# Order edges in the attention stage: weight sums behind a residual addition, two layer norm squares behind accumulator copies

## The chip, the cores and the metric

The kernel runs on one core of one Trainium2 chip. The metric is the time of one execution in device microseconds; every number called a time below is a median of several executions. The profile's own span of one execution is about 1.8 us shorter than its time (739.5 us against 741.27 us for the profiled run before), and its time axis starts at its first instruction. All runs used here are of the undisturbed ("fast") state.

## The reference, cut to what matters

A transformer block: layer norm, linear attention with 32 heads, an output projection added to the input, a second layer norm, and a gated ReLU MLP added again. S = 2048 tokens, D = 1024, F = 3584, all bf16.

```
x = A_x
h  = x + attention(layernorm(x), wqkv, wo)          # out = num / den, then @ wo
h2 = h + relu_gated_mlp(layernorm(h), W_gate, W_up, W_down)
```

## The kernel before

The kernel has three long stages that run into each other on TensorE (PE in the profile): k, v and most of the q projection (0 to 150 us), attention for 16 tiles of 128 tokens with the rest of the q projection (to 207 us) and the first MLP products between them (150 to 290 us), and the rest of the MLP (290 us to the end). All large products use Strassen's scheme: 7 products instead of 8, for which sums of the operands are made ahead on VectorE (DVE), and intermediate accumulators are copied out of PSUM (the memory, in banks, into which PE accumulates) by ScalarE (ACT).

The change touches the middle stage. Tiles are numbered 0 to 15 in the order in which they are worked on. For each, `nd` makes numerators and denominators and divides them (DVE, o_sb), a DMA transposes the result, `wo_h` multiplies by wo (PE, "attn") and adds x (DVE, line L560, one addition for each half); then the second layer norm needs the sum of squares (ACT, "square", L570), is applied (L574), and a DMA transposes the result (hn). For tiles 4 to 7 and 12 to 15 DVE then makes the "left sums" (L117 to L120), which the MLP's Strassen products need. L12 is line 12 of the kernel's own file; the change inserts lines, so that L727 of the kernel before is L729 after, and L736 is L738.

```python
def snap(v, nm, bank=A):                     # in strassen(): accumulator bank v to SBUF
    ...
    with tc.high_priority():
        nc.scalar.copy(out=snaps[nm, v], in_=bank[v][:])          # ACT, L154
...
for j in range(2):                           # in wo_h(): 8 attn matmuls, then
    with tc.high_priority():
        nc.vector.scalar_tensor_tensor(out=h_sb[...], in0=ps[:], scalar=1.0, in1=h_sb[...],
                                       op0=ALU.mult, op1=ALU.add, accum_out=tot[:, j:j + 1])   # L560
...
nc.vector.tensor_scalar(out=nmean, in0=tot[:, 0:1], scalar1=tot[:, 1:2], ...)                   # sm, L568
nc.scalar.activation(out=st["hn"][:], in_=h_sb[:], func=ACT.Square, bias=nmean, ...)            # L570
...
LAG = (0, 1, 1, 2, 4)                        # nd, oT, x_in, wo_h, hn_T of tile n: step n + LAG
def attn_step(step): ...                     # also left_sums(...) for tiles 4-7 and 12-15
...
flow = [...]                                 # four early MLP "quads", six pieces each
for step in range(QSTEPS + 2, ready):
    if step == QSTEPS + 2:
        flow.pop(0)()                        # the first quad's first product
    attn_step(step)
late_sums.pop()()                            # the first quad's eight weight sums (DVE, tg and tu)
for n in range(steps):
    attn_step(ready + n)
    for p in flow[...]:
        p()
```

An early quad multiplies two weight tiles (tg/wg and tu/wu, "v" = 0 and 1) by hn. Its products go to two A banks, two E banks and one D bank. Product m1 goes to A; its copy must be out before m6 is accumulated into the same bank; the same holds between m7 (copy "u3") and m4.

What each engine executes, and in which order, is decided by a scheduler at compile time from priorities and expected times. An order edge tells that scheduler "this instruction behind that one". Between two instructions of one engine it puts no semaphore into the program.

## Time and profile before

| | before |
|---|---|
| time, median of 3 runs at the prediction | 740.93 us (740.51 to 741.72) |
| span of the profiled execution | 739.5 us |
| PE busy | 724.0 us, 98% |
| waits of PE in 120 to 300 us, listed | 3.4 us |

The head of the profile's page of the kernel before: busy microseconds of each engine, share of the span, number of instructions.

```profile
span 739.5 us, 10552 instructions
PE 724.0 (98%) x3967; PEld 382.7 (52%) x4020; DVE 563.7 (76%) x992; ACT 321.5 (43%) x580; POOL 5.6 (1%) x44
```

PE is the bound: only its idle time can be won. (53 of its 4020 matmul records are missing from this trace, which is why a group of four sometimes shows as x3.) The list of waits of PE between 120 and 300 us, kernel before: who waited for whom, microseconds in total, times, longest.

```profile
PE attn L557 <- DVE o_sb L534: 1.0, 3, 0.5
PE Aq L727 <- ACT m L154: 0.9, 1, 0.9
PE attn L557 <- DVE x_res L560: 0.7, 1, 0.7
PE nd L527 <- DVE o_sb L534: 0.5, 1, 0.5
PE Aq L727 <- ACT u L154: 0.3, 1, 0.3
```

The second and the last line are the targets of the edges on the squares. The timeline of ACT, kernel before (start, duration, engine, line, operation, output<-input, and in brackets the idle time before it and what ended it):

```profile
261.57 0.59 ACT L154 COPY m<-Aq 128x512 f32<-128x512 f32 x1 [2.71 <-PE Aq L727]
263.31 1.15 ACT L570 ACTIVATE hn<-x_res,sm 128x1024 bf16<-128x1024 bf16 x1 [1.15 <-DVE sm L568]
264.36 0.19 ACT L570 ACTIVATION_READ_ACCUMULATOR hn<-x_res,sm 128x1 f32 x1
264.45 0.56 ACT L154 COPY m<-Aq 128x512 f32<-128x512 f32 x1
...
273.04 0.59 ACT L154 COPY u<-Aq 128x512 f32<-128x512 f32 x1 [4.88 <-PE Aq L727]
274.18 1.15 ACT L570 ACTIVATE hn<-x_res,sm 128x1024 bf16<-128x1024 bf16 x1 [0.56 <-DVE sm L568]
275.24 0.19 ACT L570 ACTIVATION_READ_ACCUMULATOR hn<-x_res,sm 128x1 f32 x1
275.33 0.56 ACT L154 COPY u<-Aq 128x512 f32<-128x512 f32 x1
```

In both places a square stands between the copies of the two banks and waits for a small DVE operation; the second copy, whose data are there, waits behind it. The timeline of PE over the same time, kernel before:

```profile
263.09 1.03 PE L727 MATMUL Aq<-hs,tg 128*128 128x512 f16 x4
265.07 1.02 PE L727 MATMUL Aq<-hs,tu 128*128 128x512 f16 x4 [0.95 <-ACT m L154]
...
273.70 1.03 PE L727 MATMUL Aq<-hn,tg 128*128 128x512 bf16 x3
274.80 0.81 PE L727 MATMUL Eq<-hs,wg 128*128 128x512 f16 x3
275.95 1.02 PE L727 MATMUL Aq<-hn,tu 128*128 128x512 bf16 x4 [0.34 <-ACT u L154]
```

The matmuls at 265.07 and 275.95 are those that waited for the late copies. And DVE, kernel before, around the weight sums: the second x addition of tile 7, the first weight sum, and the first x addition of tile 8.

```profile
206.46 0.68 DVE L560 SCALAR_TENSOR_TENSOR x_res<-attn,x_res 128x512 bf16<-128x512 f32 x1
...
209.00 0.42 DVE L636 TENSOR_TENSOR tg<-wg 128x512 f16<-128x512 bf16 x1
...
212.35 0.69 DVE L560 SCALAR_TENSOR_TENSOR x_res<-attn,x_res 128x512 bf16<-128x512 f32 x1
```

### The profile page before, as it was taken

What the parts mean: (1) busy time and instruction counts of PE and PEld (TensorE: products, weight loads), DVE (VectorE), ACT (ScalarE), POOL (GpSimd) and SP (SyncE); (2) the same over time, 40 slices, a digit from 0 to 9 for tenths busy, and PEclk for the clock granted to TensorE, in tenths of its full rate; (3) what the DMA queues carried; (4) which work ended last, traced back from release to release, by engine and by line L of the source; (5) the groups of instructions that cost most, each with busy time, mean ns of one, the idle gap of its engine ahead of it and who ended that gap; (6) DMA issues with size and microseconds to landing.
All of it is one profiled execution on the core that took longest, in us unless ns stands there. A gap on an engine that the chain in (4) does not pass through costs nothing.

```text
span 739.5 us, 10552 instructions
## 1 busy us (share of the span) xinstructions
PE 724.0 (98%) x3967; PEld 382.7 (52%) x4020; DVE 563.7 (76%) x992; ACT 321.5 (43%) x580; POOL 5.6 (1%) x44
## 2 busy tenths in 40 slices
PE   8999999999999999999999999999999999999997
PEld 3444555444444444444444444444444458888566
DVE  5997644676798767778778777877786479996797
ACT  4877554778887644434344444444445120000000
POOL 0000000000000000000000000000000000000000
PEclk9999999999999999999999999999999999999999
DMA  9666002169987426164638359575583399987822
GB/s 315 153 145 170 1 1 67 48 149 218 237 168 181 124 73 206 43 193 134 198 117 242 110 177 283 171 219 194 170 277 121 129 398 339 331 288 299 295 76 82
DMA packets 146594, 132.02 MB, mean 179 GB/s; under 512 B 50928, under 2 KB 128112, under 8 KB 146544
## 3 DMA queue, kind: packets, MB, share of 16 engines
q1 hardware_dynamic: 135536, 123.30, 55.4%
q10 hardware_dynamic: 11008, 8.06, 3.4%
q8 instruction: 31, 0.51, 0.3%
q14 instruction: 19, 0.16, 0.1%
HBM read 79.95 MB, written 39.85 MB: 162 GB/s over the span
## 4 chain that ended last, share of the span: by engine, by line
PE 78%; DVE 8%; ACT 7%; DMA 5%; issue 1%; SPq 0%; DVEq 0%; POOL 0%; ACTq 0%
PE accA L821 22%; PE accY L821 8%; PE accX L821 8%; PE accA L1153 8%; PE Aq L314 3%; PE accA L982 3%; PE attn L557 3%; PE accX L1153 3%; PE Aq L454 3%; PE accY L1153 2%; DMA hn<-hn 2%; ACT hn L570 2%; PE Eq L314 2%; PE accY L982 2%; PE accX L982 2%
## 5 line engine op out<-in xcount | busy, mean ns | idle before, releaser
L831 ACT ACTIVATE gu<-gu 128x512 bf16<-128x512 bf16 x72 | 45.4, 631 | 131.4 <-DVE gu L830 131.4
L826 ACT COPY snap<-accA 128x1024 f32<-128x1024 f32 x72 | 72.5, 1008 | 36.4 <-PE accA L821 36.3
L821 PEld LDWEIGHTS <-tu 128*128 128x128 f16 x384 | 37.6, 98 | 45.3
L821 PEld LDWEIGHTS <-tg 128*128 128x128 f16 x384 | 37.6, 98 | 45.3
L557 PE MATMUL attn<-wo_mem,oT 128*128 128x512 bf16 x247 | 58.1, 379 | 2.3 <-DVE o_sb L534 1.0
L830 DVE TENSOR_TENSOR gu<-accY,snap 128x1024 bf16<-128x1024 f32 x36 | 43.9, 1220 | 10.0 <-ACT snap L826 10.0
L821 PE MATMUL accA<-hn,tu 128*128 128x512 f16 (+1 forms) x192 | 49.3, 379 | 0.0
L821 PE MATMUL accA<-hn,tg 128*128 128x512 f16 (+1 forms) x192 | 49.3, 379 | 0.0
L830 DVE TENSOR_TENSOR gu<-accX,snap 128x1024 bf16<-128x1024 f32 x36 | 43.9, 1219 | 6.3 <-PE accX L821 3.7
L154 ACT COPY u<-Aq 128x512 f32<-128x512 f32 x54 | 31.1, 580 | 36.2 <-PE Aq L314 19.3
L1153 PEld LDWEIGHTS <-x 128*128 128x128 f16 (+1 forms) x448 | 43.8, 98 | 5.5
L821 PEld LDWEIGHTS <-wg 128*128 128x128 bf16 x288 | 28.2, 98 | 34.0
L821 PEld LDWEIGHTS <-wu 128*128 128x128 bf16 x288 | 28.2, 98 | 34.0
L557 PEld LDWEIGHTS <-oT 128*128 128x128 bf16 x256 | 24.6, 97 | 32.2 <-issue 4.1
L834 DVE TENSOR_TENSOR hq<-gu 128x512 bf16<-128x512 bf16 x48 | 20.3, 423 | 14.3 <-ACT gu L831 14.2
L314 PEld LDWEIGHTS <-xT 128*128 128x128 bf16 (+1 forms) x192 | 18.6, 98 | 23.8 <-issue 2.4
L534 DVE TENSOR_TENSOR o_sb<-nd,rd 128x384 bf16<-128x384 f32 (+1 forms) x48 | 23.2, 509 | 8.6 <-ACT rd L533 6.6
L1153 PEld LDWEIGHTS <-xs 128*128 128x128 f16 x280 | 27.4, 98 | 3.2
L982 PEld LDWEIGHTS <-x 128*128 128x128 bf16 (+1 forms) x168 | 16.5, 98 | 19.6
L560 DVE SCALAR_TENSOR_TENSOR x_res<-attn,x_res 128x512 bf16<-128x512 f32 x32 | 22.0, 686 | 6.1 <-PE attn L557 5.9
L1159 DVE TENSOR_TENSOR snap<-accA,u 128x1024 f32<-128x1024 f32 x16 | 19.5, 1220 | 8.0 <-PE accA L1153 7.9
L821 PE MATMUL accA<-hn,wu 128*128 128x512 bf16 x96 | 24.6, 379 | 0.0
(234 smaller groups left out, 1406.1 us busy)
## 6 DMA issues: line engine op xcount, KB each, us to landing
x<-x_dram SPq DMA_DIRECT2D x17, 896.0 KB, 8.1
x_dram<-hq SPq DMA_DIRECT2D x28, 512.0 KB, 3.0
wg<-in_B_W_gate_dram SPq DMA_DIRECT2D x14, 512.0 KB, 5.1
wu<-in_B_W_up_dram SPq DMA_DIRECT2D x14, 512.0 KB, 7.3
wraw<-in_B_W_down_dram SPq DMA_DIRECT2D x14, 512.0 KB, 4.8
x_dram<-hq SPq DMA_DIRECT2D x28, 256.0 KB, 2.5
t_dram<-wt SPq DMA_DIRECT2D x28, 256.0 KB, 2.2
xd<-x_dram SPq DMA_DIRECT2D x6, 896.0 KB, 7.3
```

The costliest lines, as they stand in the source:

```text
L154: nc.scalar.copy(out=snaps[nm, v], in_=bank[v][:])
L314: nc.tensor.matmul(ps[:], lhsT=left[m - 1][:, kc, r + v * P:r + (v + 1) * P], rhs=right[m - 1][:, kc, :], start=(start and kc == 0), stop= ...
L454: nc.tensor.matmul(ps[:], lhsT=rq[m - 1][:, kc, (c + v) * P:(c + v + 1) * P], rhs=left[m - 1][:, kc, :], start=(start and kc == 0), stop=( ...
L534: nc.vector.tensor_tensor(out=ov[:, c0:c0 + n], in0=ndv[:, :, 0:P].rearrange("p k (h e) -> p k h e", h=HPC), in1=rd[:, 0:n, :].unsqueeze(3 ...
L557: nc.tensor.matmul(ps[:], lhsT=st["oT"][:, c, :], rhs=wo_sb[:, c, j * NW:(j + 1) * NW], start=(c == 0), stop=(c == KC - 1))
L560: nc.vector.scalar_tensor_tensor(out=h_sb[:, j * NW:(j + 1) * NW], in0=ps[:], scalar=1.0, in1=h_sb[:, j * NW:(j + 1) * NW], op0=ALU.mult, ...
L821: nc.tensor.matmul(ps[:, v, :], lhsT=w[v][n - 1][:, kc, :], rhs=left[n - 1][:, kc, :], start=(t is not None and kc == 0), stop=(kc == KH - ...
L826: nc.scalar.copy(out=st[nm][:], in_=halves(st["A"]))
L830: add(out=g[:], in0=halves(st[nm]), in1=st[base][:], op=ALU.add)
L831: nc.scalar.activation(out=g[:, 0, :], in_=g[:, 0, :], func=ACT.Relu)
L982: nc.tensor.matmul(ps[:, t * NW:(t + 1) * NW], lhsT=x_tile(n, s, kh)[:, f, (t0 + t) * P:(t0 + t + 1) * P], rhs=w_tile(n, kh)[:, f, :], sta ...
L1153: nc.tensor.matmul(pv[:, tt, :], lhsT=left(m)[:, f, tt * P:(tt + 1) * P], rhs=right(m)[:, f, :], start=(t is not None and f == 0 and tt % ...
```

## The change

Two kinds of edges: the first quad's weight sums behind the x addition of tile 7 (`order[STS - 1]`, with STS = 8), and the squares of the last two tiles behind the copies of the third quad's second banks. The diff, with mere plumbing cut (`...` marks cuts, here and in the profiles):

```diff
-                nc.scalar.copy(out=snaps[nm, v], in_=bank[v][:])
+                copies[nm, v] = nc.scalar.copy(out=snaps[nm, v], in_=bank[v][:])
 ...
-                    nc.vector.scalar_tensor_tensor(out=h_sb[:, j * NW:(j + 1) * NW], in0=ps[:], scalar=1.0,
+                    added[t] = nc.vector.scalar_tensor_tensor(out=h_sb[:, j * NW:(j + 1) * NW], in0=ps[:], scalar=1.0,
 ...
-            nc.scalar.activation(out=st["hn"][:], in_=h_sb[:], func=ACT.Square, bias=nmean, scale=1.0, accum_out=var)
+            squared[t] = nc.scalar.activation(out=st["hn"][:], in_=h_sb[:], func=ACT.Square, bias=nmean, scale=1.0, accum_out=var)
 ...
-    late_sums.pop()()
+    with tc.issue_after(added[order[STS - 1]].ins):
+        late_sums.pop()()
 ...
+    for t, copy in ((order[-2], ("m1", 1)), (order[-1], ("u3", 1))):
+        tc.add_manual_dep(squared[t].ins, quad_copies[2][copy].ins.name,
+                          mybir.DependencyInfo(mybir.DependencyClass.NoSync, mybir.DependencyReason.DATA),
+                          reason="order")
```

No instruction is added or removed.

More of the change, by code (lines that the diff above doesn't have):

```diff
@@ L142, in hold, with strassen @@
         nc.gpsimd.tensor_copy(out=dst, in_=src)
-    def strassen(pool, work, mm, fin, sbufs=3, late=False):
+    def strassen(pool, work, mm, fin, sbufs=3, late=False, copies={}):
         A, E, snaps = {}, {}, {}
@@ L509, in block_kernel @@
     pieces = [(c, min(GPB, KC - c)) for c in range(0, KC, GPB)]
-    held = []
+    held, added, squared = [], {}, {}
     def attn_stages(t):
@@ L718, in early_sums @@
         return [load, lambda: None, lambda: None, lambda: hh_sums_a(st[0], 0, f), lambda: hh_sums_b(st[0], 0, f)]
+    quad_copies = [{} for f in range(NE)]
     def early_quad(s, fc, w):
@@ L742, in fin @@
                 nc.sync.dma_start(out=raw_dram[q][:, fc, :], in_=d[:])
-        return strassen(pspool, mwork, mm, fin, 4)
+        return strassen(pspool, mwork, mm, fin, 4, False, quad_copies[fc])
     def all_sums(wt, fi):
```

## The prediction

> **What bounds the kernel now.** TensorE. The page's busy times give PE 724.0 us of a 739.5 us span (98%), DVE 76%, ACT 43%; the chain that ended last is 78% PE. From 277 us on PE is full (the stretches show 49.79 of every 50 us), so an earlier start there should come out whole at the end. The waits of PE in 120 to 300 us (attention and the first quads) are only 3.4 us: attn for DVE o_sb 1.0, Aq for ACT m 0.9, attn for DVE x_res 0.7, nd for DVE o_sb 0.5, Aq for ACT u 0.3. That is all the change can win; it adds and removes no instruction, only order edges on one engine, without semaphores.
>
> **Edge on the squares.** The timeline shows ACT idle for 1.15 us until DVE's small sm operation; then it runs the square of the last tile but one at 263.31 (1.15 us), and only then copies the second m1 bank of the third quad (264.45). That bank's matmuls ended near 262.4, so a ready copy stood behind a waiting square: the Trainium skill ("PSUM — Partial Sum Buffer", "Engine vs sequencer instructions") says "ScalarE/VectorE/GpSimdE queues are strict FIFO", and this trace agrees (those 1.15 us). The matmul at 265.07 waited 0.95 us. With the edge the copy (0.58 us) fits into the idle time, the square is not delayed, and the 0.95 go. Likewise the last tile's square (274.18) stands before the copy of u3 (275.33), and the matmul at 275.95 waited 0.34. The square slips by at most 0.3 us; what hangs on it (the left sums at 281.65) is needed only after 290. Sum: 1.29 us. Part may come back as a new wait: quad four's tu sum on DVE (280.46 plus 0.42) ends just before its matmul (281.34), and DVE moves up by less than PE; estimate 0 to 0.4 us.
>
> **Edge on the weight sums.** The addition of tile 7 (eighth of sixteen pairs in the timeline) is at 206.46 on DVE. The first quad's eight sums run from 209.00 to 220.9: already behind it. So I expect this edge to do nothing. What PE waited for at 213.10 (0.67 us) and perhaps at 214.17 (0.48 us) was tile 8's first addition (212.35), held up by five of these sums (0.33 us apart) and left sums. If, against this, the edge pushes the sums behind tile 8's additions, up to 1.15 us more are won, at the risk that the first tg matmul (219.25) waits. I give that 30%.
>
> **Sum.** 740.93 - 1.29 + 0.2 - 0.3 x 0.9 = about 739.6 us; range 738.4 to 740.9. The three runs before spread by 1.2 us, so the gain is near the noise. Chances: faster by over 2% 0.005, within 2% 0.99, slower by over 2% 0.005.
>
> **What would show it.** Right: PE's waits for ACT m (0.9) and ACT u (0.3) are gone, and the copies stand before the squares on ACT; the waits for x_res (0.7) and o_sb (0.5) near 213 us stay; the first accA matmul moves from 289.97 to about 288.7; the later stages are unchanged. Wrong: a new PE wait on DVE's tu sums near 280 us, or accA starting earlier without the end moving.
>
> **What would make it wrong.** The compile-time scheduler orders the instructions anew: an edge can reshuffle others in 200 to 290 us and open or close waits of a few tenths; or the sums do move; or a DMA (hn transposes) rather than PE sets the start of the next stage.

## The result

| | before | after |
|---|---|---|
| time, median of 6 runs each | 740.58 us (739.56 to 741.72) | 739.07 us (738.55 to 740.33) |
| ratio, 95% interval | | 0.9981 (0.9968 to 0.9994) |
| span of the profiled execution | 739.5 us | 737.3 us |

A ratio here and below is worked out from all fast runs of both kernels in the same rounds, so it is not quite the ratio of the medians. The measured 739.07 us lies in the predicted range, 0.5 us under the 739.6 us that the prediction named. At 2% the two kernels count as the same. The head of the page, kernel after:

```profile
span 737.3 us, 10605 instructions
PE 724.7 (98%) x4020; PEld 382.1 (52%) x4020; DVE 563.8 (76%) x992; ACT 322.4 (44%) x580; POOL 5.6 (1%) x44
```

The waits of PE between 120 and 300 us, kernel after:

```profile
PE attn L557 <- DVE x_res L560: 1.3, 1, 1.3
PE attn L557 <- DVE o_sb L534: 1.1, 4, 0.5
PE nd L527 <- DVE o_sb L534: 0.5, 1, 0.5
```

Both waits of Aq for ACT are gone; the wait for x_res is 0.6 us longer. ACT, kernel after:

```profile
261.06 0.59 ACT L154 COPY m<-Aq 128x512 f32<-128x512 f32 x1 [2.69 <-PE Aq L729]
261.93 0.59 ACT L154 COPY m<-Aq 128x512 f32<-128x512 f32 x1 [0.28 <-PE Aq L729]
262.81 1.15 ACT L570 ACTIVATE hn<-x_res,sm 128x1024 bf16<-128x1024 bf16 x1 [0.30 <-DVE sm L568]
...
271.42 0.59 ACT L154 COPY u<-Aq 128x512 f32<-128x512 f32 x1 [3.96 <-PE Aq L729]
272.29 0.59 ACT L154 COPY u<-Aq 128x512 f32<-128x512 f32 x1 [0.28 <-PE Aq L729]
272.99 1.15 ACT L570 ACTIVATE hn<-x_res,sm 128x1024 bf16<-128x1024 bf16 x1
```

The second copy fits into time in which ACT had been idle. The square of tile 14 is not delayed at all: it still waits 0.30 us for its DVE operation. PE, kernel after:

```profile
262.59 1.03 PE L729 MATMUL Aq<-hs,tg 128*128 128x512 f16 x4
263.45 1.03 PE L729 MATMUL Aq<-hs,tu 128*128 128x512 f16 x4
...
272.08 1.03 PE L729 MATMUL Aq<-hn,tg 128*128 128x512 bf16 x4
272.95 1.03 PE L729 MATMUL Aq<-hn,tu 128*128 128x512 bf16 x4
273.81 1.03 PE L729 MATMUL Eq<-hs,wg 128*128 128x512 f16 x4
...
275.54 1.03 PE L729 MATMUL Aq<-hn,wg 128*128 128x512 bf16 x4
276.60 1.02 PE L729 MATMUL Aq<-hn,wu 128*128 128x512 bf16 x4
```

**How to size a stall of PE.** Four matmuls of 512 columns without a stall take 0.865 us from start to start (262.59 to 263.45 and on, 0.216 us each), although each is drawn 0.38 us long: the drawn end lies 0.16 us after the next could start. The idle time in brackets is counted from the drawn end. So a wait listed as 0.95 us cost 265.07 - 263.09 - 0.865 = 1.11 us, and the one listed as 0.34 cost 275.95 - 274.80 - 3 x 0.216 = 0.50 us. And 273.70 to 274.80 is 0.24 us longer than four matmuls need (the x3 is one missing record), though no wait is listed there at all. The Trainium skill ("Perfetto Trace Analysis", section "Per-engine timelines", on the Tensor Engine) says why one should be careful here: the profiler "**estimates** the end time from instruction size + SBUF delay". Each of the 384 matmuls accA<-hn,tg and accA<-hn,tu is drawn with exactly 379 ns, while they follow each other at 216 ns.

On this scale the change takes away 1.11 + 0.24 + 0.50 = 1.85 us. It adds one new stall: 276.60 - 275.54 - 0.865 = 0.20 us. Net 1.65 us. That is to be compared with the stretch from the third quad's first matmul to the first matmul of the MLP stage (the first accA): 289.97 - 260.50 = 29.47 us before, 287.84 - 260.00 = 27.84 us after, 1.63 us less. From that matmul to the last one the two traces have the same 445.30 us, so what is won at 275 us arrives whole at the end.

The other 0.5 us of the 2.2 us between the two spans were there before the third quad started (260.50 and 260.00), and have nothing to do with these edges. Nearly all of it comes from two accidents of the two executions. First, PE's clock at the start. Of the first 15 us, kernel before and then kernel after: busy us (instructions) of PE, PEld (PE's weight loads), DVE, ACT and POOL, then the granted clock (PEclk), the busy share of DMA and its GB/s.

```profile
0.00:15.00 15.00, 11.71 (x47) 5.12 (x48) 7.27 (x16) 4.55 (x9) 1.84 (x23) 0.89 0.90 303
```

```profile
0.00:15.00 15.00, 11.15 (x52) 5.01 (x53) 8.46 (x19) 5.67 (x12) 1.84 (x23) 1.00 0.90 304
```

The clock was 0.89 in one and 1.00 in the other, and the first attn matmul started at 158.23 and 156.96 us: 1.27 us. Experiments 1 and 10 below show that this belongs to the execution and not to the kernel: laid beside the trace of run 1, which has the same instructions and a clock of 1.00, the trace before loses 1.8 us between 5 and 13 us, where its matmuls start 0.427 us apart instead of 0.216, and from there to the first attn matmul the difference stays between 1.7 and 1.8 us. Second, a wait at 213 us (x_res) that costs PE 0.83 us in the trace before and 1.50 us in the trace after, which took 0.67 us back; the last 0.1 us lies in smaller gaps. That wait too varies between executions of the same program (experiments 1, 2 and 10).

### The profile page after: what moved, and what is told of

The parts are those of the page before. It is cut to its first block, busy times and chain, and to the rows that moved or that the text cites. A ratio compares the mean times of both kernels' runs of the same rounds, so it can differ in the third digit from the quotient of the medians.

```text
span 737.3 us, 10605 instructions
## 1 busy us (share of the span) xinstructions
PE 724.7 (98%) x4020; PEld 382.1 (52%) x4020; DVE 563.8 (76%) x992; ACT 322.4 (44%) x580; POOL 5.6 (1%) x44
## 4 chain that ended last, share of the span: by engine, by line
PE 82%; DVE 8%; DMA 5%; ACT 4%; issue 1%; SPq 0%; DVEq 0%; POOL 0%; ACTq 0%
PE accA L828 22%; PE accY L828 8%; PE accX L828 8%; PE accA L1160 8%; PE attn L557 5%; PE Aq L314 3%; PE accA L989 3%; PE accX L1160 3%; PE Aq L454 3%; PE accY L1160 2%; PE Aq L729 2%; PE Eq L314 2%; PE accY L989 2%; PE accX L989 2%; PE Eq L454 1%; PE Eq L729 1%
## 5 line engine op out<-in xcount | busy, mean ns | idle before, releaser
L828 PE MATMUL accA<-hs,tg 128*128 128x512 f16 x96 | 24.6, 379 | 0.0
```

Source lines behind the costliest of these rows:

```text
L828: nc.tensor.matmul(ps[:, v, :], lhsT=w[v][n - 1][:, kc, :], rhs=left[n - 1][:, kc, :], start=(t is not None and kc == 0), stop=(kc == KH - ...
```

## The experiments

Ten kernels ran, each five rounds, on chips shared with the kernel before. "Stretch A" is the time from the third quad's first matmul to the first accA matmul; "stretch B" that from the first attn matmul to the first accA matmul. Both are read as starts of PE's matmuls from the traces, one trace for each kernel, and the start-up clock doesn't enter into them. How far each can be trusted is shown by kernels with the same instructions: stretch A is 29.47 and 29.49 (before, run 1), and 27.84, 27.84 and 27.93 (change, runs 2 and 10), so it repeats to 0.1 us; stretch B is 131.75 and 132.59, and 130.88, 129.97 and 130.90, so it differs by up to 0.93 us where nothing was changed. All ten outputs were correct.

| run | edit | ratio to before (95%) | median us | stretch A | stretch B |
|---|---|---|---|---|---|
| before | | | | 29.47 | 131.75 |
| change | | 0.9981 (0.9968 to 0.9994) | 739.07 | 27.84 | 130.88 |
| 1 | sums edge only | 1.0012 (0.9990 to 1.0034) | 740.63 | 29.49 | 132.59 |
| 2 | both squares only | 0.9979 (0.9959 to 0.9999) | 738.60 | 27.84 | 129.97 |
| 3 | square of tile 14 only | 0.9988 (0.9970 to 1.0006) | 739.81 | 28.84 | 131.56 |
| 4 | square of tile 15 only | 0.9996 (0.9976 to 1.0015) | 739.76 | 28.71 | 131.91 |
| 5 | change, sums behind tile 8 | 0.9985 (0.9969 to 1.0000) | 739.44 | 27.63 | 131.58 |
| 6 | change, left sums of 5 later | 0.9990 (0.9974 to 1.0006) | 739.54 | 28.46 | 131.42 |
| 7 | 5 and 6 together | 0.9987 (0.9969 to 1.0006) | 739.34 | 27.63 | 131.24 |
| 8 | change, left sums of 5 and 7 later | 0.9964 (0.9948 to 0.9981) | 738.17 | 27.63 | 130.22 |
| 9 | change, left sums of 7 later | 0.9977 (0.9961 to 0.9994) | 739.21 | 27.79 | 130.71 |
| 10 | the change again | 0.9966 (0.9949 to 0.9983) | 738.68 | 27.93 | 130.90 |

The intervals are about as wide as the effect. The three of the change's instructions (the change, runs 2 and 10) all lie below 1 and that of run 1 includes 1, but the times alone could not have told the other variants apart. What tells them apart is stretch A, single gaps, and the order of the instructions.

**The theory:** the edges on the squares are the whole change, the edge on the sums is idle. **The first rival:** the sums edge has a share, since PE does wait near 213 us for an x addition that stands behind the sums.

### 1. The edge on the weight sums alone

```diff
-    for t, copy in ((order[-2], ("m1", 1)), (order[-1], ("u3", 1))):
+    for t, copy in ():
```

> Only the edge on the weight sums. Theory (the sums edge is idle): the listing of each engine's instruction order, waits included, is the same as without it, so this is a second copy of the kernel before: ratio 1.000 within noise, and 29.47 us from the third quad's first matmul to the first accA matmul, as before. Rival (the sums edge gives a part of the gain, up to the 1.15 us that PE waits near 213 us): ratio 0.9985 to 0.999, and the waits for x_res and o_sb near 213 us shorter.

Before it ran, the listing of each engine's instructions in order, waits on semaphores included, was laid beside that of the same source without any edge: on PE, DVE, ACT, POOL and SP the two were the same. The programs built from this run's kernel and from the kernel before are equal too, instruction by instruction. The two traces agree: 3967 matmul records of PE in the same order in both.

So this is the kernel before under another name, and its measured ratio of 1.0012 (0.9990 to 1.0034) is a measure of the noise. Stretch A is 29.49 us, as before. The sums already stood behind tile 7's addition; an edge that demands what is already so changes nothing. The trace of this run also shows the accidents named above in a program that is the same: the clock of the first 15 us was 1.00, the first attn matmul came at 156.43 instead of 158.23 us, and the gap near 213 us was 1.50 instead of 0.83 us.

### 2. The edges on the squares alone

```diff
-    with tc.issue_after(added[order[STS - 1]].ins):
+    if True:
         late_sums.pop()()
```

> Only the edges on the two squares. Theory: this is the whole change; 27.84 us from the third quad's first matmul to the first accA matmul (29.47 before), ratio 0.998, as the whole change. Rival (the sums edge has a share): a smaller gain than the whole change, 0.3 to 0.5 us.

Stretch A is 27.84 us, the same as with the whole change, and the listing of every engine is the same as that of the whole change: without the edge on the sums it is the same program. The rival has fallen.

### 3 and 4. One square at a time

Both are without the edge on the sums, as run 2.

```diff
-    for t, copy in ((order[-2], ("m1", 1)), (order[-1], ("u3", 1))):
+    for t, copy in ((order[-2], ("m1", 1)),):          # run 3
+    for t, copy in ((order[-1], ("u3", 1)),):          # run 4
```

> Only the edge on the square of the last tile but one. Theory (a stall costs PE the gap between matmul starts, 1.33 instead of 0.216 us, so 1.11 us and not the listed 0.95): 28.36 us from the third quad's first matmul to the first accA matmul (29.47 before), ratio 0.9985. If the listed idle time counts: 28.52 us. If the scheduler's other moves matter, anything else.

> Only the edge on the square of the last tile. Theory: the gaps of 0.24 and 0.50 us between matmul starts go, 0.20 us come back where the fourth quad's second m1 matmul waits for a DVE multiply that reads its bank: 28.93 us from the third quad's first matmul to the first accA matmul (29.47 before), ratio 0.9993. If only the listed 0.34 counts: 29.13 us. The 1.11 us gap of the last tile but one stays.

Run 4 took 0.76 us off stretch A, somewhat more than expected: the gaps of 0.24 and 0.50 us are gone, and the new one of 0.20 us did not come. So 0.74 us is the size of that stall, not the listed 0.34. Run 4's other place still has its stall, 1.09 us between matmul starts. The unlisted 0.24 us has its explanation in the order: with the square in the way, the scheduler expected the copy to be late and put three Eq matmuls in front of the waiting Aq ones, and these had to wait for a DVE addition that reads their bank until 274.75 us (0.05 us before their start). DVE of the kernel before:

```profile
274.06 0.68 DVE L736 TENSOR_TENSOR gu<-Eq,u 128x512 bf16<-128x512 f32 x1
```

With the edge they stand behind again. (That the scheduler's expected time moved them is a reading of the new order; only the order itself and the wait are shown.)

Run 3 took only 0.63 us off, and 1.11 had been expected. The stall of tile 14's copy is gone, but the gap before the Eq matmuls grew from 0.24 to 0.72 us. DVE of run 3:

```profile
270.28 0.43 DVE L117 TENSOR_TENSOR hs<-hn 128x512 f16<-128x512 bf16 x1 [1.07 <-DMA hn<-hn]
...
271.75 0.69 DVE L560 SCALAR_TENSOR_TENSOR x_res<-attn,x_res 128x512 bf16<-128x512 f32 x1
...
272.62 0.68 DVE L738 TENSOR_TENSOR gu<-Eq,u 128x512 bf16<-128x512 f32 x1
```

PE came 1.1 us earlier, but DVE stood at the left sums of tile 14 until their transpose had landed: they started 10.60 us after the third quad's first matmul, against 10.75 us in the kernel before, only 0.15 us earlier. The additions for PE queued behind them: the one that the Eq matmuls wait for ends at 273.30 us, and they start at 273.35. So 0.48 us of the gain turned at once into a longer wait on another engine's queue. The two edges together do better (1.63) than the sum of each alone (0.63 + 0.76 = 1.39), since with the second edge those Eq matmuls no longer stand in PE's way.

### 5. The weight sums behind tile 8's addition, which PE does wait for

The prediction gave a 30% chance to the sums moving behind tile 8's additions, and up to 1.15 us to that. This run makes it so.

```diff
-                    added[t] = nc.vector.scalar_tensor_tensor(
+                    added[t, j] = nc.vector.scalar_tensor_tensor(
-    with tc.issue_after(added[order[STS - 1]].ins):
+    with tc.issue_after(added[order[STS], 0].ins):
```

> The whole change, but with the weight sums behind tile 8's first x addition, which PE waits for near 212 us. Theory (the five sums ahead of that addition, some 1.7 us of DVE, make PE wait 0.8 to 1.5 us there): that gap between attn matmuls falls under 0.3 us. But DVE is full from 205 to 221 us, so the same sums then come too late for the first quad's tg and tu matmuls near 219 us, and 1 to 1.5 us come back there: ratio to the kernel before 0.997 to 0.999, no clear gain over the change. Rival (DVE has room): both gone, first attn matmul to first accA matmul 128.5 us instead of 130 to 130.9, ratio 0.996.

The sums moved, but the gap near 212 us did not fall under 0.3 us; it is still 0.97 us. DVE of run 5:

```profile
205.18 0.42 DVE L117 TENSOR_TENSOR hs<-hn 128x512 f16<-128x512 bf16 x1 [2.02 <-DMA hn<-hn]
...
206.12 0.68 DVE L560 SCALAR_TENSOR_TENSOR x_res<-attn,x_res 128x512 bf16<-128x512 f32 x1
...
211.14 0.43 DVE L217 TENSOR_SCALAR e<-e 128x1024 bf16<-128x1024 bf16 x1 [0.94 <-ACT e L216]
211.48 0.68 DVE L560 SCALAR_TENSOR_TENSOR x_res<-attn,x_res 128x512 bf16<-128x512 f32 x1
```

With the sums away, DVE idles 0.94 us in front of the same addition, because the operation before it waits for an exponential on ACT. Most of the sums' time had been time in which the addition could not have started anyway. Not all of it: from tile 7's second x addition to tile 8's first it is 5.36 us here (206.12 to 211.48) against 5.89 us in the kernel before (206.46 to 212.35) and in the change (206.10 to 211.99). So the sums held it for 0.53 us, about a third of the 1.50 us gap that the change has when the transpose lands as late as here. And the second half of the expectation held in kind, at half the size (0.61 us, not 1 to 1.5): PE's second tg product now waits 0.61 us between matmul starts (219.85 us, listed as a wait of Aq for DVE tg of 0.4). Stretch B is 131.58 us, no better than with the change. So the prediction's reading of that wait, "held up by five of these sums", was wrong for most of it.

### 6 and 7. The left sums that hold DVE until a transpose lands

In the trace after, the left sums of tile 5 make DVE idle for 1.76 us at 205.16 us, with tile 7's second x addition behind them (206.10):

```profile
205.16 0.43 DVE L117 TENSOR_TENSOR hs<-hn 128x512 f16<-128x512 bf16 x1 [1.76 <-DMA hn<-hn]
```

That addition starts a chain: square on ACT, then the copies and the exponential behind it on ACT, then tile 8's addition on DVE.

```diff
-                    left_sums(hnT[n // STS], hns[n // STS], ...)
+                    with tc.issue_after(added[order[STS - 1]].ins) if n == STS - 3 else ExitStack():
+                        left_sums(hnT[n // STS], hns[n // STS], ...)
```

> The whole change, and tile 5's left sums, which hold DVE for 1.0 to 1.8 us until a transpose lands, ordered behind tile 7's second x addition. Theory (that wait at the head of DVE's queue, set by a DMA's time, is what makes the gap near 212 us, and makes it vary from 0.8 to 1.5 us between runs): DVE no longer idles there, the gap goes or falls under 0.3 us, first attn matmul to first accA matmul about 129 us, ratio to the kernel before about 0.996. Rival (the five sums alone make the gap): the gap stays near 0.8.

> Both: weight sums behind tile 8's first x addition, and tile 5's left sums behind tile 7's second. Theory: no more gap at tile 9's attn than with the left sums alone, and the sums late again, so not better than the left sums alone, up to 1 us worse. Rival: additive, 1 us better than either.

(Run 7 joins this edit with that of run 5.) Run 6: the gap near 212 us fell to 0.32 us, with five of the sums still in front of tile 8's addition. So the wait at the head of DVE's queue for the transpose made most of that gap, not the sums. The traces in which nothing was moved there say the same: where these left sums start 47.3 us after the first attn matmul the gap is 0.83 and 0.79 us (before, run 2), at 47.9 it is 1.23 (run 3), and from 48.1 to 48.4 it is 1.49 or 1.50 (the change, runs 1, 4, 9 and 10). But stretch B did not shorten to the expected 129 us (131.42). A new gap of 1.37 us opened at 217.89 us, and the scheduler, which orders everything behind such an edge anew, made small ones elsewhere: stretch A grew from 27.84 to 28.46 us, with gaps of 0.39 and 0.36 us that the change does not have. DVE of run 6, and then the matmul that waited:

```profile
216.61 0.43 DVE L117 TENSOR_TENSOR hs<-hn 128x512 f16<-128x512 bf16 x1 [1.31 <-DMA hn<-hn]
...
217.29 0.55 DVE L534 TENSOR_TENSOR o_sb<-nd,rd 128x384 bf16<-128x384 f32 x1
```

```profile
217.89 0.33 PE L527 MATMUL nd<-kvz,pq_mem 128*128 128x132 bf16 x3 [1.21 <-DVE o_sb L534]
```

It is the same pattern one transpose later: DVE, now earlier, runs into the left sums of tile 7 before their data are there, and what PE needs stands behind them. Run 7, with both moves, has a gap of 1.83 us for o_sb at 220.53 us and is no better (131.24, well within what stretch B varies); its profiled execution had an unrelated stall of PE of some 3.4 us at 72 us, which is why only the stretches are used.

### 8, 9 and 10. The left sums of tile 7 as well

```diff
+                    behind = {STS - 3: added.get(order[STS - 1]), STS - 1: divided.get(order[STS + 3])}.get(n)
+                    with tc.issue_after(behind.ins) if behind is not None else ExitStack():
                         left_sums(hnT[n // STS], hns[n // STS], ...)
```

(`divided[t]` is the last o_sb multiply of a tile. Run 9 has only the second entry of the table, run 10 is the change unedited.)

> The whole change; tile 5's left sums behind tile 7's second x addition; tile 7's left sums behind the o_sb multiplies of tile 11. Theory (after tile 5's left sums are out of the way, the next wait for a transpose at the head of DVE's queue, tile 7's left sums for 1.31 us at 216.6 us, holds the o_sb multiplies that PE waits for, the 1.37 us gap near 218 us): that gap goes, first attn matmul to first accA matmul 129.8 to 130.3 us (131.42 with tile 5's alone), ratio to the kernel before 0.997 to 0.998. Rival (the wait moves on to the first tg matmul, which needs tile 7's left sums themselves): the gap only changes its place and the stretch stays near 131 us.

> The whole change, and only tile 7's left sums behind the o_sb multiplies of tile 11. Theory: in the change as it is these sums do not wait for their transpose (DVE reaches them late, at 218.3 us), so nothing is won here: first attn matmul to first accA matmul 130 to 131 us as with the change, ratio 0.998.

> The change once more, beside the two others on one chip: ratio to the kernel before 0.998; 27.84 us from the third quad's first matmul to the first accA matmul; 130 to 131 us from the first attn matmul to the first accA matmul, depending on when tile 5's transpose lands (gap of 0.8 to 1.5 us near 212 us).

Run 8: the 1.37 us gap is gone, what remains near there is 0.34 us before the first tg matmul, and the x_res wait no longer appears in PE's list. Stretch B is 130.22 us, as expected, and 0.66 to 0.68 us shorter than the change's 130.88 and 130.90; but the third trace of the same instructions, run 2 with its early transpose, has 129.97. Run 9 wins next to nothing alone, as expected: without the first move DVE is late enough for the transpose to have landed. So the two waits form a chain, and moving only the first shifts the stall to the second.

Whether run 8 is a better kernel than the change is not settled by the times. Its median is 0.5 us lower in the same rounds (738.17 against 738.68), and its ratio to the kernel before is 0.9964 against 0.9966: intervals that overlap almost wholly. It is the lowest median of all, against 740.67 for the kernel before in those rounds. The traces do not settle it either: 0.7 us better than the change with a late transpose, 0.25 us worse than with an early one. Shown is that the 1.37 us gap of run 6 goes; a gain over the change is not shown.

Run 10 repeats the change under the start-up clock of the kernel before: granted clock 0.89 in the first 15 us, first attn matmul at 158.23 us in both. Its span is 738.6 us, 1.3 us more than the other profile of the same program, and stretch A is 27.93 us.

## Why the prediction was right

- **PE bounds, and an earlier start comes out whole: right.** From the first accA matmul to the last matmul all traces of these kernels agree to 0.1 us, most of them at 445.30 us.
- **The edge on the squares removes both Aq waits, and costs the squares nothing: right.** The copies stand first, the first square keeps its wait for sm, and the last square starts 0.03 us after the end of its sm operation, exactly as before the change (the prediction allowed a slip of 0.3).
- **Its size, 1.29 us: too small.** It was the sum of listed idle times, 0.95 + 0.34. From start to start the stalls are 1.11 and 0.50 us, and 0.24 us more belonged to matmuls that had been pulled forward, where nothing was listed: 1.85 us together.
- **Up to 0.4 us comes back as a new wait: the size was right (0.20 us), the place was not.** It was to be the fourth quad's tu sums on DVE. These were ordered anew and made no wait. The new stall is its second m1 matmul at 276.60 us, whose bank a DVE multiply reads until 275.87 + 0.68 = 276.55 us.
- **The edge on the weight sums does nothing: right,** and shown twice, by the listing and by run 1.
- **The 30% alternative: its premise failed.** "Held up by five of these sums" explains only 0.53 us of the gap at 213 us: run 5 took the sums away and 0.97 us of 1.50 stayed, run 6 left them and it fell to 0.32 us.
- **The first accA matmul "from 289.97 to about 288.7": measured 287.84,** but 0.50 us of that was there at the third quad already, so the change moved it by 1.63 us.
- **The total of 739.6 us** (1.33 us less than 740.93) is near the measured 739.07 (1.51 less than 740.58, or 0.19% by the ratio), for the partial reason that the undersized gain and the 0.27 us set aside for an edge that does nothing partly cancel. The net gain in the trace, 1.63 us, would be a ratio of 0.9978; the intervals of the three measured ratios of these instructions (0.9981, 0.9979, 0.9966) include it. So the times show a gain but not its size: the first interval alone allows 0.4 to 2.4 us. That the predicted total came so near is in part luck.

A general check of the queue rule that the prediction rested on: the Trainium skill ("PSUM — Partial Sum Buffer", section "Engine vs sequencer instructions") says that these engines' queues are strict first in, first out. All cases here agree: ACT idle 1.15 us with a ready copy behind a square, DVE idle 1.07 us (run 3), 0.94 us (run 5) and 1.31 us (run 6) with work for PE behind the waiting instruction.

## What to carry to other kernels

In a kernel whose matmul engine is 98% busy, look for an instruction at the head of an in-order queue that waits while a ready one stands behind it; letting the ready one pass cost nothing here, and what it removed was the gap between matmul starts, less one matmul's pitch (0.76 us measured in run 4 for 0.24 + 0.50), not the listed idle time (0.34). Before adding an order edge check in the trace that the order is not already so, and afterwards compare the instruction orders: identical listings settle in seconds what times with a spread of 0.3% cannot. When one head-of-queue wait is removed, ask at once which wait the now earlier engine runs into next: in run 3 nearly half of the gain (0.48 of 1.11 us) was lost behind the next transpose, and in run 6 all of it (1.18 us won near 212 us, 1.37 us lost near 218 us).

## What the Trainium skill lacked or had wrong

- "Perfetto Trace Analysis" (section "Optimization Strategy") says to find the gaps between slices. That undercounted on PE: a wait of 0.95 us between slices cost 1.11 us, one of 0.34 cost 0.50, and gaps of 0.24 and 0.20 us from start to start hardly show between slices. The page has the reason (an estimated end) but not this consequence.
- "TensorE: Matmul & The Clock Gate" (section "What's actually happening") says that the penalty at the start is under 1% of a typical kernel's span and varies between runs. This agrees (1.8 of 740 us is 0.24%), but for small changes it needs a warning: the program before started attention at 158.23 or 156.43 us, that of the change at 158.23 or 156.96, with a granted clock of 0.89 or 1.00 in the first 15 us. Those 1.3 to 1.8 us are as large as the whole effect measured here.
- No page that I found says how far a wait moves on when it is removed at the head of an in-order queue. Here removing one of 1.76 us (run 6) opened one of 1.37 us on PE, and 0.48 of 1.11 us came back in run 3.
